# When the next layer's input blocks are built: last step of a pass, later weight stores, sums moved in a fused attention, MoE and GELU kernel

## The chip, the cores and the metric

The kernel runs on one core of a Trainium2 chip. The metric is device microseconds of one execution; the time before is the median of three runs. A second source is the profile of one execution, with its trace: the start and end of every instruction on TensorE (PE, matrix products), VectorE (DVE), ScalarE (ACT), GpSimd (POOL), and every DMA, all of which SyncE (SP) issues here from one queue, in order.

## The reference

Three stages follow each other, all in float32.

```python
q_s = softmax(q, over head_dim);  k_s = softmax(k, over the sequence)   # 4 batches, 8 heads, 576 x 64
attn = q_s @ (k_s^T @ v)                                  # per batch and head
x = attn as [2304 tokens, 512]
p = probs / sum(probs)
x = sum over 4 experts of p[:, e] * (relu(x @ w1[e]) @ w2[e])           # w1: 512 x 1024, w2: 1024 x 512
h = x @ w_in                                                            # 512 x 2048
out = (h * sigmoid(1.702 * h)) @ w_out                                  # 2048 x 512
```

w_in and w_out arrive as 64-bit floats. The kernel turns them into 32-bit ones itself ("decode").

## The kernel before

**Passes and units.** The tokens are worked on in two halves of 1152. Each layer goes over its weights once for each half, so there are four passes: MoE first half, MoE second half, GELU layer first half, GELU layer second half. (The prediction numbers them 1 to 4.) A unit is a slice of 256 hidden columns with its weights w1 (512 x 256) and w2 (256 x 512). A MoE pass has 16 units, a GELU pass 8; they are numbered 0 to 47, so passes begin at units 0, 16, 32 and 40. Each unit has two steps, one for each part of the tokens of a half (`PAIRS`): part 0 with 2*256 tokens, part 1 with 2*320. (The prediction calls these parts "half 0" and "half 1" where it speaks of x blocks.) `step` writes the instructions of one step in five stages; a unit thus has ten stage slots.

**First product.** x @ w1 is made by Strassen's scheme with seven products (`m1` to `m7` in `mm1`), on quarter blocks of w1 (a11, a12, a22 and the sums s1 to s4) and of x (b11, b21, b22 and the sums t1 to t4). `STAGES` says which products, evictions (`p1c`, `u2c`, `u3c`: ScalarE copies; `p1a`, `u3a`, `u2a`: VectorE adds), and activations (`r`, `l`: high and low part of relu; `g`, `k`: sigmoid and gate) stand in which stage. Every operand is kept as a high part, rounded to the format that TensorE takes at full rate, and a low part, the rest; each product is three matmuls, high by high, high by low, low by high. The high part is a ScalarE copy; the low part is a subtraction on VectorE (x, hidden values) or GpSimd (weights).

**Second product.** `mm2` multiplies the hidden values (h_hi, h_lo) by w2, one tile of 128 tokens at a time, in the stages of the step after; VectorE adds the product into acc. After the last unit of a MoE pass, `to_x2` transposes acc on TensorE, in the first unit of the next pass, and ScalarE copies it into xf, where it waits to be a later pass's input.

**Blocks of x.** `blocks` makes high and low parts of the x blocks from xf. The sums t1 to t4 are made in place in xf by four GpSimd subtractions, in the order St1, St3, St2, St4. `blocks_x` yields one entry of `BLOCK_STAGES` per stage. It is started after the step of part i in the last unit of a pass, so part 0 is built during the last unit's second step and part 1 during the first step of the next pass. The tiles come from a pool `xps[i]` of 14 buffers that share one tag.

**Weights.** Each weight part is made once (`hi_w1`, `lo_w1`, `hi_w2`, `lo_w2`), stored to DRAM (`store_part`), and loaded again in the layer's next pass (`new_part`). Stores wait in a list. `put_away(2)` issues all but the last two whenever one is added, and `put_away(0)` issues all of them ahead of every load. Units 0 to 2 (`AHEAD`) are worked on in the opening with the plain eight products, so their sums s1 to s4 do not exist until pass 2, where they are made for the first time; in pass 2 these units stand at places 5, 8 and 11 of 16. Unit m's weights are prepared in the stages of unit m-1 (`prepare`, with `TWO` as the plan).

**Background work.** One background generator advances by one `yield` in each stage (`pump`). In pass 1 it is `attention`, for the eight pairs of heads of the second half of the tokens; a pair goes through the 14 entries of `TURNS`, one per stage, and a new pair begins every 14. There `kdg` makes dg, a diagonal tile, on VectorE; `ks` multiplies it by ones on TensorE, which spreads the maxima over partitions; `ksv` subtracts them. In pass 2 it is `decode_all`: 32 pieces of w_in and w_out, each some seven VectorE instructions and one GpSimd addition over five stages, started after `LEAD` = 5 stages.

**Order.** Up to the step `AUTO` (the first step of unit 33) the instructions of each engine run in the order in which the program writes them (`manual_schedule`); the opening follows a list written by hand (`START`). After `AUTO` the framework orders them.

## Time and profile before

| | us |
|---|---|
| median of three runs | 1275.12 |
| lowest and highest run | 1274.0, 1275.17 |
| the profiled execution, by the same clock | 1273.28 |
| its span, first instruction to last | 1271.5 |
| TensorE busy | 1233.1 |
| VectorE busy | 925.7 |
| ScalarE busy | 501.5 |
| GpSimd busy | 383.9 |
| mean granted TensorE clock, as a share of full speed | 0.993 |

Busy times overlap: the engines run side by side and wait for each other by semaphores. Busy time of TensorE does not show whether the clock was at full speed; the granted clock of a stretch does (1.00 is 2.4 GHz, 0.5 is 1.2 GHz).

### The profile page before, as it was taken

Reading aid. Unit: us, or ns where it says so; the run is one execution under the profiler, and the core shown is the slowest. Engines: PE = TensorE matmul, PEld = TensorE weight load, DVE = VectorE, ACT = ScalarE, POOL = GpSimd, SP = SyncE. Lnnn points to the kernel's source line nnn. Section 1 sums busy time; section 2 is a strip of 40 time slices with the busy share of each in tenths; the row PEclk is TensorE's granted clock in tenths of the full one; section 3 lists DMA queues with packets and bytes.
Section 4 is the critical chain, followed back from the end, with each engine's and each line's share of the span. In section 5 each row is a group of like instructions: output and inputs, shape, how many; then the busy total and the mean of one; then the engine's idle time right before and its main releaser. Section 6 shows DMA issues by size and latency. Waiting matters only on the chain.

```text
span 1271.5 us, 20359 instructions
## 1 busy us (share of the span) xinstructions
PE 1233.1 (97%) x7358; PEld 1101.4 (87%) x7358; DVE 925.7 (73%) x1694; ACT 501.5 (39%) x1227; POOL 383.9 (30%) x407
## 2 busy tenths in 40 slices
PE   7999999999999998999999999998999999999998
PEld 7889979889889987898889889886898997999997
DVE  8973766677776578888999989559576679466665
ACT  5543333444434444222222222226754555533342
POOL 4430534344544432113131221018643633000000
PEclk9999999999999998999999999999999999999999
DMA  9765555545554353574756565533553534542432
GB/s 242 232 216 173 185 166 166 187 139 185 183 165 162 130 186 129 177 230 163 248 172 222 200 224 166 174 125 104 197 198 124 186 138 143 168 129 92 154 96 75
DMA packets 122484, 214.50 MB, mean 169 GB/s; under 512 B 29328, under 2 KB 49296, under 8 KB 122384
## 3 DMA queue, kind: packets, MB, share of 16 engines
q1 hardware_dynamic: 122384, 213.20, 51.6%
q8 instruction: 58, 0.95, 0.3%
q14 instruction: 42, 0.34, 0.1%
HBM read 130.06 MB, written 83.10 MB: 168 GB/s over the span
## 4 chain that ended last, share of the span: by engine, by line
PE 81%; DVE 11%; DMA 3%; issue 2%; SPq 1%; POOL 1%; ACT 0%; POOLq 0%; ACTq 0%; DVEq 0%
PE po L749 42%; PE px L638 20%; PE pz L638 10%; PE py L638 5%; DVE acc L761 2%; DVE h_lo L690 2%; PE px L343 1%; DMA prn<-in_moe_domain_probs 1%; PE p L366 1%; DMA w<-k_w 1%; PE cc L638 1%; DVE u L668 1%; SPq L195 1%; PE cd L638 1%; PE cb L638 1%
## 5 line engine op out<-in xcount | busy, mean ns | idle before, releaser
L749 PE MATMUL po<-w,h_hi 128*128 128x512 f32 x1728 | 544.6, 396 | 6.0 <-DMA w<-k_w 2.9
L749 PE MATMUL po<-w,h_lo 128*128 128x512 f32 x864 | 339.1, 393 | 6.9 <-DVE h_lo L690 4.6
L749 PEld LDWEIGHTS po<-w,h_hi 128*128 128x128 f32 x1728 | 302.4, 189 | 47.5 <-issue 3.6
L761 DVE SCALAR_TENSOR_TENSOR acc<-po,pr,acc 128x512 f32<-128x512 f32 x270 | 201.5, 746 | 111.2 <-PE po L749 110.4
L749 PEld LDWEIGHTS po<-w,h_lo 128*128 128x128 f32 x864 | 163.0, 189 | 48.5 <-DVE h_lo L690 8.2
L97 ACT COPY u<-px 128x256 f32<-128x256 f32 (+1 forms) x180 | 72.0, 400 | 275.1 <-PE px L638 273.6
L770 DVE TENSOR_TENSOR acc<-po,acc 128x512 f32<-128x512 f32 x126 | 86.6, 687 | 50.4 <-PE po L749 50.4
L668 DVE TENSOR_TENSOR u<-pz,u 128x256 f32<-128x256 f32 (+1 forms) x180 | 81.3, 452 | 56.2 <-ACT u L97 44.5
L576 POOL TENSOR_TENSOR s<-s,s 128x256 fp32r<-128x256 f32 x93 | 73.7, 794 | 125.7 <-ACT s L570 124.8
L576 POOL TENSOR_TENSOR a<-ra,a 128x256 fp32r<-128x256 f32 x71 | 55.3, 782 | 130.1 <-ACT a L570 123.8
L97 ACT COPY p<-px 128x256 f32<-128x256 f32 x90 | 35.8, 398 | 136.6 <-PE px L638 136.5
L589 POOL TENSOR_TENSOR w<-rc,w 128x512 fp32r<-128x512 f32 x46 | 60.4, 1318 | 73.3 <-ACT w L583 73.2
L690 DVE SCALAR_TENSOR_TENSOR h_lo<-u,h_hi 128x256 fp32r<-128x256 f32 (+1 forms) x116 | 71.9, 620 | 0.0
L684 ACT ACTIVATE h_hi<-u 128x256 fp32r<-128x256 f32 (+1 forms) x116 | 51.7, 446 | 49.9 <-DVE u L668 49.9
L638 PE MATMUL px<-t4hg,a 128*128 128x256 f32 (+1 forms) x256 | 61.8, 297 | 2.0 <-ACT u L97 1.9
L638 PE MATMUL pz<-t1hg,s 128*128 128x256 f32 (+1 forms) x256 | 62.6, 300 | 0.0
L638 PE MATMUL px<-t2hg,s 128*128 128x256 f32 (+1 forms) x256 | 62.4, 299 | 0.0
L638 PE MATMUL pz<-b22hg,s 128*128 128x256 f32 (+1 forms) x256 | 61.8, 297 | 0.5 <-DVE u L668 0.4
L638 PE MATMUL px<-b11hg,a 128*128 128x256 f32 (+1 forms) x256 | 61.7, 296 | 0.0
L638 PE MATMUL py<-b21hg,a 128*128 128x256 f32 (+1 forms) x256 | 61.6, 296 | 0.0
L638 PE MATMUL px<-t3hg,s 128*128 128x256 f32 (+1 forms) x256 | 61.5, 296 | 0.0
L441 POOL TENSOR_TENSOR xf<-xf 128x512 f32<-128x512 f32 (+1 forms) x26 | 43.4, 1669 | 46.3 <-DVE b11lg L437 29.8
(247 smaller groups left out, 2665.3 us busy)
## 6 DMA issues: line engine op xcount, KB each, us to landing
w<-k_w SPq DMA_DIRECT2D x54, 512.0 KB, 4.5
k_w<-w SPq DMA_DIRECT2D x48, 512.0 KB, 4.2
k_s<-s SPq DMA_DIRECT2D x96, 256.0 KB, 2.7
a<-k_a SPq DMA_DIRECT2D x84, 256.0 KB, 3.0
s<-k_s SPq DMA_DIRECT2D x84, 256.0 KB, 3.2
k_a<-a SPq DMA_DIRECT2D x75, 256.0 KB, 3.0
ra<-in_moe_w SPq DMA_DIRECT2D x19, 512.0 KB, 4.1
rc<-in_moe_w SPq DMA_DIRECT2D x16, 512.0 KB, 4.5
```

Source lines behind the costliest of these rows:

```text
L97: (eng.copy if eng is A else eng.tensor_copy)(o, i)
L195: S_.dma_start(out=a[:, :, h * D : (h + 1) * D], in_=src[b, 2 * j + h].rearrange("(p c) d -> p c d", c=NCH),)
L441: (eng or G).tensor_tensor(out=o, in0=a, in1=b, op=ALU.subtract)
L576: eng.tensor_tensor(out=lo, in0=block_w(m, x), in1=hi.bitcast(F32), op=ALU.subtract)
L589: eng.tensor_tensor(out=lo, in0=raw[m, 1][:, c, :], in1=hi.bitcast(F32), op=ALU.subtract)
L638: T.matmul(ps, a[:, kk, :], b[:, kk, :], start=(start and n == 0), stop=(stop and n == 5), skip_group_check=True,)
L668: return lambda _: V.tensor_tensor(out=y[o], in0=y[ps], in1=y[o], op=ALU.add)
L684: A.activation(hi, y[c], AF.Relu)
L690: V.scalar_tensor_tensor(out=lo, in0=y[c], scalar=0.0, in1=hi.bitcast(F32), op0=ALU.max, op1=ALU.subtract)
L749: T.matmul(ps, a, b, start=(n == 0), stop=(n == 3 * FT - 1))
L761: V.scalar_tensor_tensor(out=acc[ti], in0=ps, scalar=pe, in1=acc[ti], op0=ALU.mult, op1=ALU.add)
L770: V.tensor_tensor(out=acc[ti], in0=ps, in1=acc[ti], op=ALU.add)
```

## The change

- Each x block has a tag of its own with two buffers (high and low); t4 shares b12's.
- `blocks_x` is started at the beginning of the last unit's step for each part, and its stages stand in a new order over seven stages: five in that step and two in the next. The sums are made in the order St1, St2, St3, St4. The wait for the rest of the background work (`pump(10000)`) comes ahead of the last unit's first step.
- The first unit of a pass has its own `STAGES`: m4 ahead of m3, m7 ahead of m6.
- A weight part that no later pass loads is not stored. The others are stored when more than two stages have gone by since they were made (`put_old`), and a load issues only the stores up to that of the same part.
- In pass 2 the units 0, 1 and 2 stand at places 11, 12 and 13, not 5, 8 and 11.
- In `TURNS`, "qe" moves between "kg kgm kdg" and "ks ksv"; a pair of heads begins every 13 stages. Decode starts after 15 stages, and is put on the list one step earlier.

```diff
@@ -77,7 +77,7 @@
     sump = ctx.enter_context(tc.tile_pool(name="sump", bufs=4))
     hp = ctx.enter_context(tc.tile_pool(name="hp", bufs=1))
     evp = ctx.enter_context(tc.tile_pool(name="evp", bufs=7))
-    xps = [ctx.enter_context(tc.tile_pool(name="xp0", bufs=14))]
+    xps = [ctx.enter_context(tc.tile_pool(name="xp0", bufs=2))]
     dram = ctx.enter_context(tc.tile_pool(name="dram", bufs=1, space=DRAM))
     psc = ctx.enter_context(tc.tile_pool(name="psc", bufs=5, space=PSUM))
     pso = ctx.enter_context(tc.tile_pool(name="pso", bufs=3, space=PSUM))
@@ -391,7 +391,7 @@
 
     KBANK = {0: ("kT0", "kT1", "kb0", "kb1"), 1: (), 2: (), 3: ()}
     TURNS = (
-        "km", "qm qs", "kg kgm kdg", "ks ksv", "qe", "ke", "qu qp qr", "qn", "pk",
+        "km", "qm qs", "kg kgm kdg", "qe", "ks ksv", "ke", "qu qp qr", "qn", "pk",
         "rz rr bd0 bd1", "t0 qT0", "t1 qT1", "px0 xf0", "px1 xf1",
     )
 
@@ -428,7 +428,7 @@
 
         def hi(m):
             X[i, m] = tuple(
-                xps[i].tile([P, 2, n], F32R, tag=f"x{i}", name=f"{m}{r}{nm}") for r in "hl"
+                xps[i].tile([P, 2, n], F32R, tag="t4" if m == "b12" else m, name=f"{m}{r}{nm}") for r in "hl"
             )
             A.copy(X[i, m][0], src[m])
 
@@ -447,8 +447,9 @@
             ops["S" + m] = lambda e, m=m: sub(m, e)
         return ops
 
+
     BLOCK_STAGES = (
-        "Hb11 Lb11 Hb21 Lb21", "St1 Hb22 Lb22", "Ht1 Lt1 St3", "St2 Ht3 Lt3", "Ht2 Lt2 St4", "Ht4 Lt4",
+        "Hb11 Lb11 St1", "Hb21 Lb21", "Ht1 Lt1 St2", "Ht2 Lt2 St3 St4", "Ht3 Lt3", "Hb22 Lb22", "Ht4 Lt4",
     )
 
     def blocks_x(g, i):
@@ -483,7 +484,7 @@
 
                 layer = moe[AHEAD:]
                 for n, x in enumerate(moe[:AHEAD]):
-                    layer.insert(5 + 3 * n, x)
+                    layer.insert(11 + n, x)
             units += [(*x, pas, i == 0, i == len(layer) - 1) for i, x in enumerate(layer)]
     NG = len(units)
     steps = [(g, 0, g) for g in range(AHEAD)] + [(g, 1, AHEAD + g) for g in range(AHEAD)]
@@ -507,7 +508,8 @@
         flat = t.rearrange("p l a b -> p (l a b)").bitcast(F32)
         u = of_unit[m]
         if again[m, x]:
-            put_away(0)
+            while any(key == (u, x) for key, *_ in stores):
+                put_away(len(stores) - 1)
             S_.dma_start(out=flat, in_=kept[u, x])
         else:
             parts[m, x] = flat
@@ -517,20 +519,29 @@
 
     def store_part(m, x):
 
-        d = dram.tile(list(parts[m, x].shape), F32, name=f"k_{x}_{m}")
-        kept[of_unit[m], x] = d
+        if not any(again.get((later, x)) and of_unit[later] == of_unit[m] for later in range(m + 1, len(insts))):
+            parts.pop((m, x))
+            return
+        d = kept[of_unit[m], x] = dram.tile(list(parts[m, x].shape), F32, name=f"k_{x}_{m}")
         put = lambda flat=parts.pop((m, x)): S_.dma_start(out=d, in_=flat)
         if m < AHEAD:
             first_stores[m, x] = put
             return
-        stores.append(put)
-        put_away(2)
+        stores.append(((of_unit[m], x), put, stage[0]))
 
     first_stores = {}
 
     def put_away(but):
         while len(stores) > but:
-            stores.pop(0)()
+            stores.pop(0)[1]()
+
+    stage = [0]
+
+    def put_old():
+
+        stage[0] += 1
+        while stores and stage[0] - stores[0][2] > 2:
+            put_away(len(stores) - 1)
 
     def load_w(m, part):
         if all(again[m, x] for x in (("w20", "w21") if part else STRASSEN if m >= 2 * AHEAD else PLAIN)):
@@ -727,8 +738,15 @@
 
     STAGES = {
         "moe": ("m1 p1c", "m2 p1a", "m3 u2c ra m4 la", "m5 u3c u3a", "m6 rb rc", "m7 u2a lb lc", "rd", "ld"),
+        "moe first": (
+            "m1 p1c", "m2 p1a", "m4 m3 u2c ra la", "m5 u3c u3a rb", "m7 u2a lb", "m6 rc lc", "rd", "ld",
+        ),
         "ffn": ("m1 p1c", "m2 p1a ga" , "m3 u2c ka m4 ra la", "m5 u3c u3a gb", "m6 kb gc",
                 "m7 u2a rb lb kc gd", "rc lc kd", "rd ld"),
+        "ffn first": (
+            "m1 p1c", "m2 p1a ga", "m4 m3 u2c ka ra la", "m5 u3c u3a gb", "m7 u2a kb gd",
+            "m6 rb lb kd gc", "kc rd ld", "rc lc",
+        ),
     }
 
     def mm2(g, ti, m, ho):
@@ -822,7 +840,7 @@
             rs = slice(r * P, (r + 1) * P)
             todo.append(decode(w_out[rs, :], wo32[rs, :], dec, f"o{r}"))
         next(todo[0])
-        yield from [None] * LEAD
+        yield from [None] * 3 * LEAD
         for n, x in enumerate(todo):
             for stage, _ in enumerate(x):
                 yield
@@ -839,7 +857,9 @@
         nxt = m + 1 if m + 1 < len(insts) else None
         plan = (ONE if len(mine) == 1 else TWO)[mine.index(steps[k_])]
         ops = mm1(g, i, m, k_ % 2 * HB)
-        st = STAGES[units[g][0]]
+        st = STAGES[units[g][0] + " first" * units[g][4]]
+        if units[g][5] and g + 1 < NG:
+            blk[0].append(blocks_x(g, i))
         for s in range(5):
             if s == 0:
                 run(ops, st[0])
@@ -855,6 +875,7 @@
             blk[0] = [x for x in blk[0] if next(x, x) is not x]
             if nxt is not None:
                 prepare(nxt, plan[s])
+            put_old()
             if mine[0] == steps[k_]:
                 if s in (1, 3) and (m, s // 2) not in W2:
                     hi_w2(m, s // 2)
@@ -935,9 +956,9 @@
 
     def begin_p1():
         bgp[0].__exit__(None, None, None)
-        xps.append(ctx.enter_context(tc.tile_pool(name="xp1", bufs=14)))
+        xps.append(ctx.enter_context(tc.tile_pool(name="xp1", bufs=2)))
         bgp[0] = tc.tile_pool(name="attn2", bufs=1)
-        bg.append(attention(heads[2 * NPR :], bgp[0].__enter__(), 14))
+        bg.append(attention(heads[2 * NPR :], bgp[0].__enter__(), 13))
 
     ops = probs_ops()
     add = lambda suffix, more: ops.update({f"{x}:{suffix}": fn for x, fn in more.items()})
@@ -987,15 +1008,13 @@
         kind, *_, pas, first, last = units[g]
         if k_ == AUTO:
             manual.__exit__(None, None, None)
-        tail = step(k_, last_of(k_ - 1), tail)
-        if last and g + 1 < NG:
-            if kind == "moe" and i == 0:
-                pump(10000)
-                bgp[0].__exit__(None, None, None)
-            blk[0].append(blocks_x(g, i))
-            if kind == "moe" and i == 0 and pas == 0:
+        if last and kind == "moe" and i == 0:
+            pump(10000)
+            bgp[0].__exit__(None, None, None)
+            if pas == 0:
                 bgp[0] = tc.tile_pool(name="dec", bufs=2)
                 bg.append(decode_all(bgp[0].__enter__()))
+        tail = step(k_, last_of(k_ - 1), tail)
     run(tail[0], tail[1][-2] + " " + tail[1][-1])
     for t in last_of(len(steps) - 1):
         for x in mm2(*t):
```

## Rows read from the trace of the kernel before

**Rows 1.** The page, part 1: busy us, share of the span, instructions.

```profile
PE 1233.1 (97%) x7358; PEld 1101.4 (87%) x7358; DVE 925.7 (73%) x1694; ACT 501.5 (39%) x1227; POOL 383.9 (30%) x407
```

**Rows 2.** Stretches by unit: length, busy us (instructions), granted clock, DMA share, GB/s.

```profile
527.18:550.80 23.62, 23.62 (x140) 21.29 (x139) 21.87 (x42) 5.48 (x14) 3.88 (x3) 1.00 0.57 184
816.94:840.56 23.62, 23.62 (x140) 21.30 (x139) 12.57 (x24) 5.49 (x14) 0.74 (x1) 1.00 0.37 125
1118.12:1141.74 23.62, 23.62 (x141) 21.30 (x139) 14.82 (x33) 9.04 (x22) 0.00 (x0) 1.00 0.37 125
467.07:503.49 36.42, 31.89 (x177) 27.09 (x175) 31.00 (x48) 17.34 (x35) 11.31 (x7) 0.91 0.31 97
865.02:901.32 36.30, 30.43 (x177) 25.99 (x175) 29.04 (x38) 23.81 (x53) 28.43 (x25) 0.95 0.45 153
1043.39:1094.50 51.11, 48.56 (x279) 42.20 (x277) 41.64 (x74) 27.13 (x62) 13.13 (x8) 1.00 0.53 160
574.42:769.70 195.28, 190.53 (x1106) 169.85 (x1105) 176.68 (x326) 47.80 (x124) 47.55 (x44) 1.00 0.60 205
```

**Rows 3.** Stretches at a lower granted clock; busy us: PE, PEld, DVE, ACT, POOL.

```profile
185.50:189.00 3.50, 3.50 (x13) 2.91 (x12) 1.67 (x4) 1.72 (x4) 0.73 (x1) 0.51 0.43 176
489.30:496.20 6.90, 6.09 (x20) 5.40 (x21) 5.45 (x11) 1.89 (x5) 0.08 (x1) 0.51 0.64 189
888.60:892.10 3.50, 3.23 (x11) 3.13 (x12) 2.76 (x5) 2.30 (x5) 3.50 (x4) 0.51 0.95 344
```

**Rows 4.** TensorE's waits from 120 us on: us in total, times, longest.

```profile
PE pb L278 <- DVE dg L274: 5.6, 3, 2.6
...
PE po L749 <- DMA w<-k_w: 2.9, 4, 1.2
```

**Rows 5.** The tile dg: how often, ns shortest/median/longest, first and last start.

```profile
L274 DVE TENSOR_SCALAR dg<-ident,gm x12: 271/288/2403, 12.5 to 406.5; 128x128 f32<-128x128 f32 x12
```

**Rows 6.** Timeline, 585.5 to 591.6 us: start, us, engine (SPq: issued by SyncE).

```profile
585.74 0.32 SPq L522 DMA_DIRECT2D k_s<-s  x1
...
586.11 0.42 SPq L511 DMA_DIRECT2D w<-k_w  x1
...
591.49 0.43 DVE L605 TENSOR_SCALAR dsi<-w64i 128x512 int32<-128x512 int32 x1 [3.25 <-DMA w64i<-in_moe_w_in]
```

**Rows 7.** The page, part 6: DMA issues, KB each, us to landing.

```profile
k_s<-s SPq DMA_DIRECT2D x96, 256.0 KB, 2.7
```

**Rows 8.** The tile xf, from which blocks are built: ns shortest/median/longest.

```profile
L441 POOL TENSOR_TENSOR xf<-xf x26: 1277/1626/2425, 51.9 to 1068.0; 128x512 f32<-128x512 f32 x13, 128x640 f32<-128x640 f32 x13
...
L437 DVE TENSOR_TENSOR b11lg<-xf,b11hg x6: 678/750/817, 459.4 to 1058.8; 128x512 fp32r<-128x512 f32 x3, 128x640 fp32r<-128x640 f32 x3
...
L437 DVE TENSOR_TENSOR t3lg<-xf,t3hg x6: 714/1384/2215, 467.1 to 1067.0; 128x512 fp32r<-128x512 f32 x3, 128x640 fp32r<-128x640 f32 x3
```

**Rows 9.** Stretches by step, around the changes of pass; columns as in rows 2.

```profile
443.45:455.40 11.95, 11.95 (x75) 10.67 (x74) 7.09 (x15) 3.62 (x9) 2.84 (x3) 1.00 0.59 198
455.40:467.07 11.67, 11.67 (x67) 10.64 (x66) 9.05 (x14) 5.56 (x13) 4.46 (x4) 1.00 0.67 225
467.07:483.27 16.20, 14.66 (x90) 12.12 (x89) 16.10 (x24) 8.49 (x17) 6.43 (x4) 1.00 0.24 83
...
852.51:865.02 12.51, 11.93 (x68) 10.57 (x66) 9.29 (x15) 6.25 (x15) 6.29 (x5) 1.00 0.37 124
...
1055.90:1070.04 14.14, 12.21 (x67) 10.48 (x66) 14.14 (x21) 7.15 (x16) 7.00 (x4) 1.00 0.68 204
```

**Rows 10.** The tile xf from 455.40 to 467.07 us: low parts of part 0.

```profile
L437 DVE TENSOR_TENSOR b11lg<-xf,b11hg x1: 678/678/678, 459.4 to 459.4; 128x512 fp32r<-128x512 f32 x1
L437 DVE TENSOR_TENSOR b21lg<-xf,b21hg x1: 682/682/682, 460.0 to 460.0; 128x512 fp32r<-128x512 f32 x1
...
L437 DVE TENSOR_TENSOR b22lg<-xf,b22hg x1: 1114/1114/1114, 462.8 to 462.8; 128x512 fp32r<-128x512 f32 x1
...
L437 DVE TENSOR_TENSOR t1lg<-xf,t1hg x1: 672/672/672, 464.9 to 464.9; 128x512 fp32r<-128x512 f32 x1
```

## The prediction

> **What bounds the kernel now.** I read the page's busy times first: TensorE is busy for 97% of the span [rows 1]. So a change pays only where TensorE stands still or runs at its lower clock. The second view is the table of stretches, cut where a weight unit begins. An ordinary unit takes 23.62 us, in the MoE layer with or without the decode of the later weights beside it, and in the other layer [rows 2]: TensorE's own pace. Longer stretches show where it loses:
>
> - First unit of pass 2: 36.42 us, nine transposed tiles among them. TensorE is idle for 36.42 - 31.89 = 4.5 us [rows 2], and 6.9 us run at 0.51 of the clock, the 1.2 GHz level [rows 3], which costs 3.5 more: 8.0 us lost.
> - First unit of pass 3: 36.30 - 30.43 = 5.9 us idle [rows 2] and 1.7 us for 3.5 us at the lower level [rows 3]: 7.6 us.
> - Last unit of pass 3 and first of pass 4: 51.11 - 2*23.62 = 3.9 us [rows 2].
> - Units 20 to 27, in which the sums of the three early units are made: 195.28 - 8*23.62 = 6.3 us [rows 2].
> - Attention for the second half of the tokens: TensorE waits 5.6 us, in three waits, for the diagonal tile "dg" [rows 4]; after the first of them 3.5 us run at 0.51 of the clock, 1.7 us lost [rows 3]: 7.3 us.
>
> Together 33.1 us lie open. Most of TensorE's other idle time is in the opening, whose written order the diff leaves alone.
>
> **Attention: a turn between "dg" and its matmul.** Before, "kg kgm kdg" and "ks ksv" are consecutive turns. "dg" takes 0.288 us at its median but 2.403 at its longest [rows 5], and the matmul behind it on TensorE stood for up to 2.6 us [rows 4]. A turn is one of the ten stage slots of a unit, 2.36 us (23.62/10). With "qe" between, the matmul is issued that much later, and 2.6 becomes 0.2. What is late next: VectorE is still held for 2.4 us, so the h_lo and acc behind "dg" come late; and "ke" now follows "ksv" after one turn instead of two. So not all comes back. Bounds: 3 us (over half returns under another name) and 7.3. I take 5.8. The skew of 13 moves the heads against the stages and lets one head's last turn meet the next one's first; I price it at nothing, within those bounds. Eight heads need 5 + 7*13 + 14 = 110 turns, and 121 slots lie before the last unit, so the pump of all that is left, now ahead of that unit, finds nothing.
>
> **Sums and stores.** A unit that prepares an early unit makes four sums, four ScalarE copies and four low parts, and stores the low parts' blocks. All DMAs stand in SyncE's one queue, in order. A store of s was issued at 585.74, once GpSimd's low part was there; right behind it came the load of w at 586.11, and a load of decode input, for which VectorE then idled 3.25 us [rows 6]. TensorE's waits for w are four, 2.9 us in all [rows 4]. The change takes out exactly these stores: nothing reads the 12 sum parts of the three early units again, so 96 stores of s [rows 7] become 84. Other stores go out three stages after their low part, when nothing is left to wait for, and a load that needs an earlier store flushes only up to that one. That clears the 6.3 us. What remains: the three early units now follow each other (units 26 to 28 prepare them), while the decode, its start put off by ten slots, runs on to the middle of unit 29. VectorE's 21.87 us in 23.62 [rows 2] leave it 1.75 us per unit. I keep 1.5 us of loss: 4.8 gained, bounds 2 and 6.3.
>
> **x blocks in the last step.** With the rotation over 14 buffers a block came back to its own buffer already, since the order was fixed; the new tags only allow another order. The work is the same: 7 ScalarE copies and 7 VectorE low parts of about 0.68 us (512 elements) or 0.81 (640), and 4 GpSimd subtractions, for each half [rows 8]. What moves is when. Before, half 0's blocks share the step that begins at 455.40, with the last unit's second half, and half 1's the step at 467.07, with the transposes and the first decode; VectorE is busy for 16.10 of 16.20 us there [rows 9]: it, not TensorE, sets the pace. After: five low parts of half 0 in the step before (7.09 + 5*0.68 = 10.5 of 11.95 us); in the next, four of half 0 go (3.15 us [rows 10]) and two of half 0 and five of half 1 come (9.05 - 3.15 + 2*0.68 + 5*0.81 = 11.3 of 11.67); the step that was overfull keeps two (1.6 us) and no decode. The blocks are needed a step later only, so no matmul waits for one directly; the reordered products of the first units (t1 ahead of t2, t4 last) cover the last two. The old readers are issued a stage or more ahead of each overwrite, so that wait costs nothing.
>
> VectorE is thus at 97% of one step, instead of overfull for two. Bounds: 0 gained, and the full 8.0. GpSimd's work lengthens VectorE's: t3's low part took 0.714 to 2.215 us [rows 8]. Four such hits of 1.2 us would make 16 of 11.67. The nearest row is the step at 455.40, with the same pair of engines at the same work and no idle TensorE [rows 9]. I take 2 us lost: 6.0 gained. At pass 3 the new weights are made in the same steps, and GpSimd has 6.29 us of work in the step at 852.51 already [rows 9]; I take 3.1 lost, 4.5 gained (bounds 0 and 7.6). Pass 4 is in the part that the framework orders by itself. Its step is filled already (14.14 us of VectorE in 14.14 [rows 9]), and VectorE's base is higher (14.82 us per unit against 12.57 [rows 2]), so a move brings little: 1.0 (bounds -3 and 3.9).
>
> The Trainium skill, SBUF — State Buffer, section "Who interferes with whom", speaks against this move: a VectorE instruction with two SBUF inputs and a GpSimd instruction that reads SBUF exclude each other, and the second to come waits for the whole of the first. The trace agrees in that low parts of one shape take three times their shortest. By that rule alone each low part could wait out a subtraction; the last rival below is this mechanism.
>
> **Sum.** 5.8 + 4.8 + 6.0 + 4.5 + 1.0 = 22.1 us. The profiled execution took 1273.28 us (span 1271.5), 1.8 under the median of 1275.12. Against its own time that is 1251.2; against the median, on which I forecast, 1253. Best bounds: 7.3 + 6.3 + 8.0 + 7.6 + 3.9 = 33.1, 1242. Worst: 3 + 2 + 0 + 0 - 3 = 2, 1273.
>
> **Rivals.**
> - The overload only moves: VectorE is overfull one step earlier, and the three changes of pass give nothing. Then 5.8 + 4.8 = 10.6 us: 1264.5. For it: 11.3 of 11.67 us without any hit. Against: the pressure spreads over three steps instead of two, and decode is out of the way. Chance 0.18.
> - Nearly all comes back, 30 us or more: 1245 or less. For it: each loss named has an edit aimed at the wait that ends last there. Against: VectorE's 93% and 97%. Chance 0.08.
> - Attention and sums give nothing, since VectorE's lateness, not the order of turns or of the queue, is behind their waits; the passes do as forecast: 1275.1 - 11.5 = 1263.6. For it: "dg" itself took 2.4 us. Against: TensorE's longest wait there ends with "dg", and the load of w stands right behind the store. Chance 0.08; together with the first rival, no change: 0.05.
> - Slower: GpSimd holds VectorE one for one. In the last MoE step four subtractions of about 2.0 us come onto 11.3: 19.3 of 11.67, 7.6 late; in the step before four of 1.4 onto 10.5: 16.1 of 11.95, 4.1 late; with a stretch at the lower clock some 14 lost for each MoE pass against 8. In the later layer, from 7.4 per step, 15 against 4. For the sums, 5.5 us more of GpSimd per early unit ((47.55 - 8*3.88)/3 [rows 2]) on 21.87 makes 3.75 lost in each of three units, 11 against 6.3. Net 6 + 6 + 11 + 5 - 5.8 = 22 us slower: 1297. It decides once more than about half of GpSimd's time falls on VectorE. Against: the step at 455.40 loses nothing. Chance 0.06.
>
> **How the numbers follow.** The forecast has 0.53 around 1253, its own range 1246 to 1260; no change from other small causes has the last 0.02. The range that leaves out 2 in 10 reaches over the two rivals near 1264 and, below, into the nearly full return: 1241 to 1266. A measurement of this kernel can tell about 0.2%, 2.6 us. Faster 0.87, same 0.07, slower 0.06.
>
> **What would show it.** Right: units 20 to 26 at 23.62 us; no wait for "dg" over 0.5 us; the first units of passes 2 and 3 near 30 us, the granted clock at 1.00 throughout; 12 stores of s fewer. Wrong: VectorE full through the last steps of passes 1 and 2, with TensorE waiting for h_lo or acc there; low parts of x near 2 us as a rule; units 26 to 29 over 25 us; new idle time in the layer that the framework orders.

## The result: 1.0% faster, and where it came from

The changed kernel takes 1261.97 us (median of four, 1261.31 to 1262.4), the kernel before 1275.14 (median of four, 1274.0 to 1275.53). That is 13.2 us less, a ratio of 0.9898 with a 95% interval of 0.9881 to 0.9915. The forecast was 1253, with 1241 to 1266: the direction was right and the size too large by 9 us. The profiled execution took 1261.31 us, its span is 1259.5.

The page of the changed kernel, parts 1 and 6, against [rows 1, 7]:

```profile
PE 1230.3 (98%) x7358; PEld 1102.1 (87%) x7358; DVE 918.9 (73%) x1694; ACT 503.9 (40%) x1227; POOL 380.8 (30%) x407
...
k_s<-s SPq DMA_DIRECT2D x84, 256.0 KB, 3.5
```

The work is the same, less 12 stores of s. The table of stretches of the changed kernel follows, columns as in [rows 2], engines in the order of [rows 1]. Its rows are: the opening; units 3 to 14; the last step of pass 1; unit 16, which begins pass 2; units 20 to 27; the last step of pass 2; unit 32, which begins pass 3; units 39 and 40, the change to pass 4.

```profile
0.00:128.24 128.24, 118.64 (x846) 107.20 (x847) 92.50 (x182) 59.30 (x134) 41.69 (x51) 0.96 0.69 199
128.24:438.48 310.24, 309.76 (x1858) 278.22 (x1857) 214.39 (x378) 127.86 (x328) 142.17 (x170) 1.00 0.54 175
450.40:462.75 12.35, 11.99 (x67) 10.56 (x66) 11.74 (x19) 6.28 (x13) 5.84 (x5) 1.00 0.63 211
462.75:492.85 30.10, 27.77 (x176) 24.76 (x175) 18.46 (x34) 14.79 (x30) 5.59 (x4) 1.00 0.33 106
564.22:754.82 190.60, 190.08 (x1106) 170.07 (x1105) 174.66 (x326) 46.48 (x120) 41.14 (x37) 1.00 0.61 201
838.90:851.41 12.51, 12.05 (x67) 10.32 (x66) 12.51 (x18) 7.04 (x15) 8.04 (x7) 1.00 0.30 105
851.41:886.12 34.71, 29.71 (x176) 25.96 (x175) 21.07 (x33) 22.55 (x49) 24.11 (x23) 0.95 0.47 167
1028.28:1082.31 54.03, 49.18 (x278) 43.62 (x277) 41.24 (x74) 27.80 (x62) 12.04 (x8) 0.97 0.51 151
```

Where [rows 2, 9] show no row of before for a term, I cut the trace of before at the same unit starts. The terms of the sum stand against the measured stretches so (us gained in the two profiled executions; a minus is a loss):

| term | forecast | measured | stretches, before and after |
|---|---|---|---|
| attention | 5.8 | 7.65 | units 3 to 14: 317.89, 310.24 |
| sums and stores | 4.8 | 3.1 | units 18 to 30: 313.38, 310.24 |
| change to pass 2 | 6.0 | 5.7 | units 15 and 16: 60.03, 54.37 |
| change to pass 3 | 4.5 | 1.4 | units 31 and 32: 60.75, 59.33 |
| change to pass 4 | 1.0 | -2.9 | units 39 and 40: 51.11, 54.03 |
| opening | 0 | -2.7 | to unit 3: 125.56, 128.24 |

With -0.3 elsewhere this is the 12.0 us between the spans. The medians differ by 13.2, between these 12.0 and the 14.7 that the table gives without the opening, whose length varies by itself (last section).

TensorE's waits from 120 us on in the changed kernel (total, times, longest), against [rows 4]. The waits for dg and for loads of w are gone (what is left for w, 0.4 us, ends with GpSimd's making of it), and the list is led by h_lo, which VectorE makes, and by the copy of u on ScalarE:

```profile
PE po L767 <- DVE h_lo L701: 7.9, 5, 4.3
PE px L649 <- ACT u L97: 4.8, 2, 3.0
PE po L767 <- DVE h_lo L705: 0.7, 1, 0.7
PE po L767 <- POOL w L600: 0.4, 1, 0.4
PE pz L649 <- DVE u L679: 0.3, 1, 0.3
```

Dg itself (tile view, against [rows 5]) is as slow at its longest as it was:

```profile
L274 DVE TENSOR_SCALAR dg<-ident,gm x12: 270/288/2387, 13.2 to 386.0; 128x128 f32<-128x128 f32 x12
```

What h_lo and u wait for is one step further back. ScalarE's waits for the blocks from 430 to 1100 us, in the kernel before and then in the changed one:

```profile
ACT t2hg L433 <- POOL xf L441: 3.2, 3, 1.4
```

```profile
ACT t2hg L433 <- POOL xf L441: 12.1, 6, 2.5
```

VectorE's wait for the same tile, in the changed kernel (none of this kind in the kernel before):

```profile
DVE t2lg L437 <- ACT t2hg L433: 7.5, 6, 1.8
```

ScalarE stands at t2's cast in all six builds of blocks, up to 2.5 us each. The timeline of the changed kernel at the start of unit 32 shows what that holds up (start, us, engine, line, what; in brackets the idle time before and its releaser):

```profile
850.96 0.81 DVE L437 TENSOR_TENSOR t1lg<-xf,t1hg 128x640 fp32r<-128x640 f32 x1
...
851.85 1.56 POOL L441 TENSOR_TENSOR xf<-xf 128x640 f32<-128x640 f32 x1 [2.55 <-DVE t1lg L437]
...
853.45 0.73 ACT L433 CAST t2hg<-xf 128x640 fp32r<-128x640 f32 x1 [2.23 <-POOL xf L441]
...
854.07 3.61 POOL L441 TENSOR_TENSOR xf<-xf 128x640 f32<-128x640 f32 x2
...
854.21 2.07 DVE L437 TENSOR_TENSOR t2lg<-xf,t2hg 128x640 fp32r<-128x640 f32 x1 [1.78 <-ACT t2hg L433]
...
856.20 0.48 DVE L679 TENSOR_TENSOR u<-pz,u 128x320 f32<-128x320 f32 x1
856.60 1.43 DVE L701 SCALAR_TENSOR_TENSOR h_lo<-u,h_hi 128x320 fp32r<-128x320 f32 x1
857.95 0.48 DVE L701 SCALAR_TENSOR_TENSOR h_lo<-px,h_hi 128x320 fp32r<-128x320 f32 x1
...
858.49 0.50 PE L767 MATMUL po<-w,h_lo 128*128 128x512 f32 x1 [4.30 <-DVE h_lo L701]
```

Read it downward. T1's low part ends on VectorE at 851.77; only then may GpSimd subtract t2 in place (t1's reader has to be done); then ScalarE casts t2; then VectorE takes t2's low part. ScalarE stood for 2.23 us and VectorE for 1.78 in the middle of it. The add into u and the h_lo values that TensorE needs are behind t2's low part in VectorE's order, and TensorE waits 4.30 us for a chain in which it has no part.

At the change to pass 4 it is ScalarE's order that holds TensorE (same view, part 1 of unit 39): the cast of t2 waits for GpSimd, the copy of u stands behind the cast, and TensorE waits for that copy.

```profile
1052.94 0.72 ACT L433 CAST t2hg<-xf 128x640 fp32r<-128x640 f32 x1 [2.50 <-POOL xf L441]
...
1053.57 0.42 ACT L97 COPY u<-px 128x320 f32<-128x320 f32 x1
...
1054.04 0.63 PE L649 MATMUL px<-t4hg,a 128*128 128x320 f32 x1 [3.03 <-ACT u L97]
```

### The profile page after: what moved, and what is told of

It reads as the page before. It is cut to its first block, busy times and chain, and to the rows that moved or that the text cites. A ratio compares the mean times of both kernels' runs of the same rounds, so it can differ in the third digit from the quotient of the medians.

```text
span 1259.5 us, 20324 instructions
## 1 busy us (share of the span) xinstructions
PE 1230.3 (98%) x7358; PEld 1102.1 (87%) x7358; DVE 918.9 (73%) x1694; ACT 503.9 (40%) x1227; POOL 380.8 (30%) x407
## 4 chain that ended last, share of the span: by engine, by line
PE 81%; DVE 10%; issue 5%; POOL 2%; DMA 1%; ACT 1%; SPq 0%; POOLq 0%; ACTq 0%
PE po L767 41%; PE px L649 19%; PE pz L649 10%; PE py L649 4%; DVE h_lo L701 2%; POOL xf L441 1%; DVE acc L779 1%; PE p L366 1%; PE px L343 1%; PE cc L649 1%; PE cd L649 1%; PE cb L649 1%; PE ca L649 1%; DMA k<-in_k 1%; PE pt L471 0%
## 5 line engine op out<-in xcount | busy, mean ns | idle before, releaser
L701 DVE SCALAR_TENSOR_TENSOR h_lo<-u,h_hi 128x256 fp32r<-128x256 f32 (+1 forms) x116 | 77.4, 667 | 0.0
L636 POOL TENSOR_TENSOR doi<-doi,dti 128x512 f32<-128x512 f32 x16 | 21.0, 1312 | 149.6 <-DVE doi L633 149.6
L441 POOL TENSOR_TENSOR xf<-xf 128x512 f32<-128x512 f32 (+1 forms) x26 | 39.9, 1545 | 80.7 <-DVE b11lg L437 64.4
```

The lines of the kernel that those rows point to most:

```text
L441: (eng or G).tensor_tensor(out=o, in0=a, in1=b, op=ALU.subtract)
L636: G.tensor_tensor(out=o, in0=o, in1=t.bitcast(F32), op=ALU.add)
L701: V.scalar_tensor_tensor(out=lo, in0=y[c], scalar=0.0, in1=hi.bitcast(F32), op0=ALU.max, op1=ALU.subtract)
```

## The experiments

The theory, **A**: t2's chain of four links (VectorE, GpSimd, ScalarE, VectorE) is given one stage slot (2.36 us) by the new `BLOCK_STAGES`, and as each engine works in order, whatever is written behind its links waits too; this ate the gain at the changes of pass. The main rival, **B**: VectorE is simply full in the last step (12.51 of 12.51 us at 838.90, 11.74 of 12.35 at 450.40), and no order of the same work helps. Other questions have theories of their own, told at each run. All ratios are against runs of the kernel before on the same chip.

**The changed kernel again** (no edit).

> The changed kernel once more, on another occasion, for the opening (everything ahead of unit 3). In the first profile of it the opening took 128.2 us against 125.6 before, with 10.2 us at the lower clock against 3.4. Theory A (the opening varies from execution to execution; its order of work is the same up to 40 us): this profile's opening may come out anywhere between 125 and 129, and the stretch from unit 3 to the end is the same as in the first profile within 0.5 us. Rival B (later stores or the other buffers lengthen the opening): 128 again with 10 us at the lower clock, median 1262.

1262.28 us (1260.66 to 1262.54), ratio 0.9908 (0.9893 to 0.9923). Units 31, 32, 39 and 40 repeat within 0.6 us each; unit 16 took 31.62, not 30.10, with a granted clock of 0.95 in it against 1.00. From unit 3 to the end it is 1.6 us longer, not the same within 0.5. So differences up to 1.5 us in one unit 16 mean nothing below where the clock differs. Two later runs in which the blocks of this stretch are built in the same way took 31.65 and 31.66 for unit 16: 30.10 is the exception. The opening took 127.81 us with 6.8 at the lower level, which by itself decides between neither of its two theories (last section).

**Attention alone**, on the kernel before:

```diff
-        "km", "qm qs", "kg kgm kdg", "ks ksv", "qe", "ke", ...
+        "km", "qm qs", "kg kgm kdg", "qe", "ks ksv", "ke", ...
-        bg.append(attention(heads[2 * NPR :], bgp[0].__enter__(), 14))
+        bg.append(attention(heads[2 * NPR :], bgp[0].__enter__(), 13))
```

> The kernel before with two parts of the change alone: qe between kg and ks in the turns, and a pair of heads every 13 stages. Theory A (the wait for dg goes): units 3 to 14 take 310.2 us together as in the changed kernel, not 317.9, and nothing else moves: 7.6 us less, median near 1267. Rival (VectorE's lateness comes back as waits for h_lo): 3 us less or none. The opening is that of the kernel before, SyncE's order included: theory A of the opening expects 125 to 129 us here too, the rival 125.6.

1267.38 us (1264.63 to 1268.45), ratio 0.994 (0.9919 to 0.996). Units 3 to 14 as in the changed kernel (table of stretches of this run):

```profile
127.60:437.80 310.20, 309.72 (x1859) 278.17 (x1858) 214.01 (x378) 127.83 (x328) 142.47 (x170) 1.00 0.53 170
```

The two edits carry the whole 7.7 us, with TensorE idle for 0.48 in 310.20. In these units nothing came back under another name. Which of the two edits carries how much wasn't separated.

**Stores alone**, on the kernel before: a part that no later pass loads is not stored; the early units stay at places 5, 8 and 11, the other stores stay as they were.

```diff
     def store_part(m, x):
+        if not any(again.get((later, x)) and of_unit[later] == of_unit[m] for later in range(m + 1, len(insts))):
+            parts.pop((m, x))
+            return
```

> The kernel before with one part of the change alone: the 12 sum parts that no later pass reads are not stored. The early units stay at places 5, 8 and 11. Theory A (the stores in SyncE's queue held up the loads behind them): units 20 to 27 take 8 times 23.62 us, 6.3 less than before, without any move of the early units; one execution near 1267. Rival B (VectorE's and GpSimd's load in those units, the move matters): units 20, 21, 23, 26 and 27 keep at least half of it, 3 us or more.

One execution: 1268.09 us. Units 20 to 27:

```profile
575.06:764.52 189.46, 189.27 (x1106) 170.18 (x1105) 175.02 (x326) 47.92 (x124) 47.35 (x44) 1.00 0.59 194
```

From 195.28 [rows 2] to 189.46: 5.8 of the 6.3 us lost there, with the same 44 GpSimd instructions and three sum-making units as before. In the kernel before, TensorE waited in these units 2.3 us for loads of w and 2.4 us for h_lo; here it waits 0.2 us, for h_lo. How SyncE's queue stood in the kernel before, from 574 to 604 us (a store of s waits for GpSimd's low part of s):

```profile
SPq L522 <- POOL s L576: 14.1, 4, 6.5
```

The stores in SyncE's queue were the cause; the making of the sums, beside decode, accounts for 0.5 us at most, and moving the early units was not needed for this.

**Decode one stage earlier**, on the changed kernel. There, units 19, 21, 23 and 25 take 24.05 us instead of 23.62, and in each of them a weight load on TensorE stands 0.6 us for h_lo. Decode's pieces repeat every four stages and the units every ten, so the two meet differently when decode begins at another stage. The theory is that this meeting makes the loss; the rival, that the denser sums or stores do.

```diff
-        yield from [None] * 3 * LEAD
+        yield from [None] * (3 * LEAD - 1)
```

> The changed kernel with the decode started after 14 stages instead of 15, nothing else. In its first profile every second unit from 18 to 28 lost 0.4 us to a late h_lo, which units of the kernel before did not. Theory A (a piece takes four stages, so the start modulo four sets which h_lo stands behind which decode instruction; 14 gives back the phase of the kernel before): those losses of 2.4 us in all go, median near 1259.5. Rival B (VectorE's load in the decode is the cause, whatever the phase): they stay, in the same or in other units, 1262.

1259.86 us (1258.85 to 1260.6), ratio 0.9891 (0.9876 to 0.9906). Unit 19 of the changed kernel, then of this run:

```profile
540.17:564.22 24.05, 23.91 (x140) 21.22 (x139) 20.83 (x42) 5.49 (x14) 3.89 (x3) 1.00 0.56 171
```

```profile
540.97:564.59 23.62, 23.62 (x141) 21.30 (x139) 21.19 (x43) 5.56 (x14) 2.58 (x2) 1.00 0.71 225
```

All of units 18 to 26 are at 23.62 us now, and no weight load waits for h_lo in them: the 0.43 us in each of four units came from the stage at which decode begins. Units 28 and 29 are at 23.62 as well (23.85 and 24.51 before this edit), and unit 27 is at 24.19 (23.98).

**Decode nine stages earlier**, on the changed kernel, to ask whether the earlier building of blocks or decode's later start gave the gain at pass 2. Decode's first instruction comes 7.0 us after the start of unit 16 in the kernel before and 19.1 after it in the changed one; here it comes 2.8 ahead of it, so earlier than in either.

```diff
-        yield from [None] * 3 * LEAD
+        yield from [None] * (LEAD + 1)
```

> The changed kernel with decode started after 6 stages instead of 15, in the last unit of pass 1, so that decode and the building of x blocks share the steps again, nothing else. Theory A (the earlier building itself gives most of what was won at the change to pass 2): unit 16 takes 30 to 32 us as in the changed kernel, unit 15 less than 1 us more. Rival B (it is decode's later start that took the load off VectorE): units 15 and 16 together lose 3 us or more against the changed kernel's 54.4.

One execution: 1263.72 us. Unit 16:

```profile
461.85:497.63 35.78, 30.66 (x176) 27.13 (x175) 28.02 (x48) 14.69 (x30) 9.50 (x6) 0.90 0.38 126
```

Units 15 and 16 take 24.27 + 35.78 = 60.05 us, as much as before (60.03), 5.7 more than after and 4.2 more than in the repeat (24.27 + 31.62): with decode in the same steps, the earlier blocks show no gain. Since decode begins here even earlier than it did before, this alone doesn't say what they would gain with decode where it was; the next run asks from the other side.

**Decode eight stages later**, on the kernel before; blocks are built as before.

```diff
-        yield from [None] * LEAD
+        yield from [None] * (2 * LEAD + 3)
```

> The kernel before with one edit: decode starts after 13 stages instead of 5, so after the change to pass 2 (a whole number of pieces later). The x blocks are built where they were. Theory B' (decode's later start gave what was won at this change of pass; the earlier run with decode after 6 stages left the changed kernel only 0.6 us there): unit 16 takes 30 to 32.5 us instead of 36.4, one execution near 1270. Theory A (the earlier building of the blocks is needed as well): unit 16 stays over 34 us.

One execution: 1267.73 us. Unit 16:

```profile
468.42:496.72 28.30, 28.03 (x176) 24.74 (x175) 21.11 (x34) 17.45 (x35) 9.31 (x5) 1.00 0.38 122
```

From 36.42 [rows 2] to 28.30: 8.1 us, all of the loss that the prediction had put at 8.0, with one number changed and no block built earlier. VectorE has 34 instructions and 21.11 us in the unit instead of 48 and 31.00: decode's share of them was the overload. Units 31 and 32, where nothing was changed, took 61.39 us here, and 59.94 with attention alone, against 60.75: the change to pass 3 varies by itself by some 1.5 us.

**T2's cast one stage later** than its subtraction, on the changed kernel (t3's subtraction moves up by two stages, t3's blocks by one):

```diff
-        "Hb11 Lb11 St1", "Hb21 Lb21", "Ht1 Lt1 St2", "Ht2 Lt2 St3 St4", "Ht3 Lt3", "Hb22 Lb22", "Ht4 Lt4",
+        "Hb11 Lb11 St1", "Hb21 Lb21 St3", "Ht1 Lt1 St2", "Ht3 Lt3", "Ht2 Lt2 St4", "Hb22 Lb22", "Ht4 Lt4",
```

> The changed kernel with another order of the block stages: the subtraction for t3 one stage after that for t1, t2's high and low part in the fifth stage, not the fourth, t3's in the fourth. Work, engines and steps are the same. Theory A (t2's chain, low part of t1 on VectorE, subtraction on GpSimd, high part on ScalarE, low part on VectorE, has one stage of 2.36 us, so ScalarE and VectorE stand still in order with evictions and h_lo behind): the waits of ScalarE for xf fall from 12 us to under 4, units 16, 32 and 39 lose 2, 4 and 3 us instead of 2.8, 7.4 and 6.8, median near 1254. Rival B (VectorE has too much work in the last step, GpSimd lengthens it): nothing that matters changes, 1261 to 1263.

1257.3 us (1256.77 to 1258.4), ratio 0.9873 (0.9858 to 0.9888). ScalarE's wait (whole run), then units 32 and 39 with 40:

```profile
ACT t2hg L433 <- POOL xf L441: 9.2, 6, 2.5
```

```profile
849.79:883.33 33.54, 30.09 (x176) 25.88 (x175) 20.10 (x33) 21.82 (x49) 22.29 (x22) 0.95 0.52 181
1025.48:1079.40 53.92, 49.07 (x279) 43.58 (x277) 41.24 (x74) 27.84 (x62) 12.03 (x8) 0.97 0.52 152
```

The same work in another order takes 5.0 us less than the repeat, so B alone doesn't hold. But it stops between the theories: the wait went down by 2.9 us only, and the change to pass 4, where the framework orders, is unmoved: there ScalarE still stands 2.50 us at t2's cast and TensorE 3.03 us for the copy of u. The edit also moves t3's subtraction on GpSimd, so it isn't the cast alone that moved.

**T2's subtraction on VectorE**, on the changed kernel: the chain loses its step over GpSimd and keeps its stages; VectorE gets more work.

```diff
-        "Hb11 Lb11 St1", "Hb21 Lb21", "Ht1 Lt1 St2", ...
+        "Hb11 Lb11 St1", "Hb21 Lb21", "Ht1 Lt1 St2@V", ...
```

> The changed kernel with the subtraction for t2 on VectorE in place of GpSimd, the stages unchanged. Theory A (the chain through GpSimd in one stage is the cost): the chain is shorter by GpSimd's queue and 0.8 to 1 us of its longer instruction, ScalarE's waits for xf fall to under 5 us, median 1256 to 1258, in spite of 0.7 to 0.8 us more of VectorE in each of six steps. Rival B (VectorE's load is the cost): six more instructions on it, 1263 to 1266.

1255.31 us (1253.89 to 1256.43), ratio 0.9859 (0.9842 to 0.9875). ScalarE's wait, then the same two stretches:

```profile
ACT t2hg L433 <- DVE xf L441: 9.6, 6, 2.5
```

```profile
848.10:881.67 33.57, 29.71 (x176) 25.99 (x175) 21.52 (x34) 22.53 (x49) 20.86 (x21) 0.95 0.48 172
1023.86:1074.93 51.07, 48.31 (x279) 42.18 (x277) 41.65 (x76) 27.62 (x62) 10.24 (x6) 1.00 0.53 161
```

7.0 us less than the repeat with more work on VectorE: against B. Units 39 and 40 take 51.07, as before the change; TensorE's waits for the copy of u in them fall from 4.8 us to 1.3. The edit also takes six subtractions off GpSimd. ScalarE still waits 9.6 us in all, more than theory A had it, so the total of that wait is a poor measure; what counts is where it falls and what is queued behind it.

**The written order kept up to unit 41**, on the changed kernel. The rival to A at pass 4 is that the framework's order, not the chain, made the loss.

```diff
-    AUTO = 2 * NPASS * len(moe) + 2
+    AUTO = 2 * NPASS * len(moe) + 20
```

> The changed kernel with the written order of instructions kept to the end of unit 41, where the changed kernel leaves the order to the framework from unit 33 on. Theory A (t2's chain in one stage costs at every change of pass; the framework only decides what stands behind it): unit 39 or 40 still loses 3 to 6 us, now to h_lo as in units 16 and 32. Rival B (the framework's own order of evictions is the cause at pass 4): units 39 and 40 lose under 2 us together, median 5 us under the changed kernel's.

1273.86 us (1271.19 to 1274.73), ratio 0.9991 (0.9979 to 1.0002). TensorE's waits from 1030 to 1095 us, and units 39 and 40:

```profile
PE po L767 <- ACT h_hi L697: 5.8, 2, 4.0
PE po L767 <- DMA w<-k_w: 4.1, 1, 4.1
```

```profile
1030.16:1094.54 64.38, 54.20 (x279) 46.96 (x277) 41.35 (x74) 28.45 (x65) 16.33 (x11) 0.89 0.47 151
```

In the written order the change to pass 4 costs 64.38 - 2*23.62 = 17.1 us, with the framework's order 6.8: the framework's order didn't make the loss, for the written one loses more. That fits neither forecast: the loss is larger than both, and TensorE's longest waits end with h_hi and with a load, not with h_lo. The run isn't clean: 4.1 us of it are a load of w that comes late in the written order, and up to 3.4 more go with the 6.8 us at the lower clock level that begin in that wait; the 9.6 without them are still more than 6.8. What makes the loss in the written order isn't shown; that t2's chain makes it in the framework's order, the run before shows.

**Combinations.** First the kernel before with the three edits alone that proved sufficient above: attention, unread parts not stored, decode eight stages later.

> The kernel before with four parts of the change's effect and none of the block's: the two attention edits, no stores of parts that nobody reads, decode after 13 stages. If the parts add up (7.5 for attention, 5.9 for the stores, 4 to 6 for decode at unit 16, nothing lost at pass 4): median 1255 to 1258, below the changed kernel by 4 to 7 us. If the earlier building of blocks carries part of the gain: 1260 or more.

1253.7 us (1253.29 to 1254.16), ratio 0.9835 (0.9818 to 0.9853): 8 us under the changed kernel without the earlier building, the age rule for stores or the moved units. The gains of the three alone were 7.3, 6.6 and 6.3 us (the last two from one execution each), 20.2 together; this is 20.3, so they add up; the median is a little under the 1255 to 1258 expected. Then the changed kernel with t2 both later and on VectorE, and decode one stage earlier:

```diff
-        "Hb11 Lb11 St1", "Hb21 Lb21", "Ht1 Lt1 St2", "Ht2 Lt2 St3 St4", "Ht3 Lt3", "Hb22 Lb22", "Ht4 Lt4",
+        "Hb11 Lb11 St1", "Hb21 Lb21 St3", "Ht1 Lt1 St2@V", "Ht3 Lt3", "Ht2 Lt2 St4", "Hb22 Lb22", "Ht4 Lt4",
...
-        yield from [None] * 3 * LEAD
+        yield from [None] * (3 * LEAD - 1)
```

> The changed kernel with three edits: t2's subtraction on VectorE, t3's a stage earlier and t2's parts a stage later, decode after 14 stages. If the chain through t2 and the phase of decode are what the changed kernel still lost (theory A), the single gains of 7 (t2 on VectorE) and 2.4 add up with a little more from the order: median 1251 to 1254. If VectorE's total is the bound at units 16 and 32 (theory B), the order adds nothing and the added instructions eat part: 1255 or more.

1251.15 us (1250.34 to 1252.53), ratio 0.9815 (0.9799 to 0.9832). ScalarE's wait and unit 32:

```profile
ACT t2hg L433 <- DVE xf L441: 4.9, 5, 1.3
```

```profile
847.32:879.21 31.89, 28.32 (x176) 24.71 (x175) 20.39 (x34) 21.82 (x49) 20.92 (x20) 1.00 0.55 190
```

With both, the wait is half of what it is with either, and units 31 and 32 give 60.75 - 56.87 = 3.9 us against before, where the forecast had 4.5; units 39 and 40 take 50.13 us and give 1.0, where it had 1.0. Last, this kernel with the blocks of pass 2 built when and in the order that the kernel before had, and decode eight stages later than before (`EARLIER` holds the `BLOCK_STAGES` of the kernel before):

```diff
-        yield from [None] * (3 * LEAD - 1)
+        yield from [None] * (3 * LEAD + 3)
...
-        for x in BLOCK_STAGES:
+        for x in EARLIER if g < 16 else BLOCK_STAGES:
...
-        if units[g][5] and g + 1 < NG:
+        if units[g][5] and 16 <= g and g + 1 < NG:
...
+        if last and g < 16:
+            blk[0].append(blocks_x(g, i))
```

> The run with t2 on VectorE, its parts a stage later, with two edits: at the change to pass 2 the blocks are built when and in the order in which the kernel before built them, and decode starts after 18 stages (one piece later than after 14). Theory B' (at that change the earlier building costs and decode's start is what helped): unit 15 at 23.6 and unit 16 at 28.3 to 29 us instead of 29.9, everything behind as in the run before; median 1249 to 1250. Rival (the earlier building helps once t2's chain is mended): unit 16 at 29.9 or more, 1251 or more.

1249.6 us (1248.71 to 1250.24), ratio 0.9803 (0.9787 to 0.9819): the lowest median of all, though the interval overlaps that of the run before it. Units 16 and 32:

```profile
462.03:490.89 28.86, 28.03 (x176) 24.76 (x175) 21.40 (x35) 17.45 (x35) 8.88 (x5) 1.00 0.37 118
...
846.34:879.01 32.67, 29.75 (x177) 25.89 (x175) 20.72 (x34) 22.34 (x49) 20.73 (x20) 0.95 0.51 186
```

Units 15 and 16 take 52.48 us together, against 53.62 in the run before it, with the granted clock at 1.00 in both. Two things differ between the two runs, so these 1.1 us don't say which of them gave it.

## Why the prediction was right, and where it failed

- **Attention**: the mechanism was right, the term too small, 7.65 for 5.8, and above its own upper bound of 7.3. "So not all comes back" was too cautious. Dg still takes up to 2.387 us, but with a turn between, TensorE waits 0.5 us in all from 130 to 436.
- **Sums and stores**: the mechanism was right, as the run with the stores alone shows (5.8 us). Of it 3.1 stand in the changed kernel. The missing 1.7 against the forecast are the 4 * 0.43 us of units 19, 21, 23 and 25, which the prediction didn't foresee: the stage at which decode begins. The 1.5 us that the prediction kept as lost late in the pass seem to be there: units 27, 28 and 29 have 0.36, 0.23 and 0.89 us over 23.62. But with decode one stage earlier 0.57 us in unit 27 is all that is left of them, so that the size agreed was in good part luck.
- **Change to pass 2**: 6.0 forecast, 5.7 measured, and the cause mostly wrong, so that the sizes agree is luck. The prediction gave the gain to blocks built a step earlier and named decode's absence ("and no decode") only beside it. Decode's start did it: alone it gives 8.1 us, and with decode pulled forward the earlier blocks give nothing. Nor are 5.7 us the usual size: with the 31.6 us that unit 16 took in the repeat it is 4.1. Nor was decode "put off by ten slots": it is put on the list five slots earlier, and starts 12.1 us, five slots, later against unit 16. Whether the earlier building gains or costs anything there with decode equally late wasn't separated. Its order costs something: unit 15 takes 24.27 us in the repeat and 23.62 with t2's cast a stage later.
- **Changes to pass 3 and 4**: here the forecast failed, by 3.1 + 3.9 = 7.0 us, nearly all that its terms miss (22.1 - 14.9 = 7.2). The step is "The blocks are needed a step later only, so no matmul waits for one directly; [...] that wait costs nothing". No matmul waits for a block, true. But the casts and low parts stand in the same in-order queues as the evictions and h_lo that matmuls do wait for, and t2's chain over VectorE, GpSimd, ScalarE and VectorE was given one slot. TensorE waits 4.3 us behind it in unit 32 and 4.8 in unit 39, and falls to the lower clock level after it: the granted clock was 0.95 in unit 32 and 0.97 over units 39 and 40, not "at 1.00 throughout". Even the 1.4 us gained at pass 3 are in doubt, since runs that build the blocks as before had 59.66 to 61.39 us there. I priced the instructions by their busy time and left out the wait between them. Splitting the chain over two stages, or taking GpSimd out of it, gives 5.0 and 7.0 us of the kernel's time back; both together with decode's earlier stage, 11. In that last version the two changes of pass give 3.9 and 1.0 us, against 4.5 and 1.0 forecast. Both mends also move work of GpSimd, which can lengthen VectorE's instructions. But it isn't less lengthening that they gave: in units 31 and 32 the time of VectorE's instructions over the shortest of their operation, tiles and shape in these runs sums to 12.4 us in the changed kernel, 12.6 in the repeat, and 12.5, 12.0 and 12.2 in the three mended ones.
- **VectorE's fill** was put at 11.3 of 11.67 us for the last step; it came out as 11.74 of 12.35 (pass 1) and 12.51 of 12.51 (pass 2). The rival "the overload only moves" (1264.5) is close to the measured time, but for another reason: it had passes 2, 3 and 4 give nothing each, and they gave +5.7, +1.4 and -2.9. Part of it holds at pass 3: at its best unit 32 has 31.89 us (the version with both mends, granted clock 1.00), 3.6 above the 28.30 that unit 16 can have with the same transposes. How much of this is VectorE's total and how much GpSimd's lengthening of it stays open; no run tells them apart.
- **One for one** (1297) did not come, as a total. In single places it is seen (below). The "three times" that the prediction read from [rows 8] compares two shapes: within one shape t3's low part spans 0.714 to 1.786 us (512 elements) and 0.810 to 2.215 (640), 2.5 and 2.7 times.

## What to carry to other kernels

When work is moved into a step with spare busy time, lay out the chain between engines as well as the busy sums: at each hop to another engine the waiting instruction stops everything written behind it (here 2.23 us on ScalarE, then 1.78 on VectorE), so a chain needs as many slots as its hops take, or fewer hops. Take each edit alone on the kernel before: three small edits gave 20 us (1273.98 to 1253.7), the full change 13. A store that waits for its producer holds back every load behind it in the queue that issues both, so data that nothing reads again isn't free to store (5.8 us here).

## What the runs showed of the hardware

**The opening varies by itself.** It takes 125.56 to 128.55 us in the profiled executions, with 3.4, 6.8 or 10.2 us of it at the lower clock level. The kernel before had 125.56 and 3.4; with nothing but decode moved, which begins 365 us after the opening ends, it had 126.88 and 3.4, and with the attention edits alone 127.60 and 6.8. The changed kernel had 128.24 and 10.2, and in the repeat 127.81 and 6.8. The first of the combinations, whose opening is written as in the kernel before, had 128.21 and 10.2. So the -2.7 us of the table can't be laid to the change. Which executions get the longer stretch at the lower level isn't explained by any run.

**Same shape, other inputs, other time.** In the tile view of the changed kernel (ns shortest/median/longest) h_lo is made with one operation in the same two shapes, from u in SBUF or from px in PSUM:

```profile
L701 DVE SCALAR_TENSOR_TENSOR h_lo<-u,h_hi x116: 405/482/2195, 139.3 to 859.6; 128x256 fp32r<-128x256 f32 x58, 128x320 fp32r<-128x320 f32 x58
...
L701 DVE SCALAR_TENSOR_TENSOR h_lo<-px,h_hi x58: 408/450/491, 140.5 to 858.0; 128x256 fp32r<-128x256 f32 x29, 128x320 fp32r<-128x320 f32 x29
```

From px it never takes more than 0.491 us; from u it takes up to 2.195. Sorted by what GpSimd did meanwhile: 19 of the 58 from px ran beside a GpSimd instruction and took at most 0.479 us. Of the 116 from u, the 75 with none beside them took at most 0.494; all that took longer, up to 2.195, are among the 41 beside one. In the timeline above, two GpSimd subtractions run from 854.07 to 857.68. Beside them t2's low part takes 2.07 us where t1's took 0.81, and h_lo from u takes 1.43 and ends just after them, where h_lo from px right behind it takes 0.48. The Trainium skill, SBUF — State Buffer, section "Who interferes with whom", states this as an exclusive lock between a VectorE instruction with two SBUF inputs and a GpSimd instruction that reads SBUF; these rows agree with it. In unit 32 it adds 1.26 + 0.95 = 2.2 us to the chain that TensorE waited for.
